# A written-out order of TensorE's jobs in place of a dispatch rule, in a fused attention and feed-forward kernel

## The chip, the cores and the metric

One core of a Trainium2 chip. The metric is the device time of one execution in microseconds (us), the median of several runs. The span in a profile is the time from the first to the last instruction of one profiled execution; the timed value is 1.7 to 2.2 us longer.

## The reference

Sigmoid attention for 8 batches of 12 heads, 448 positions, 64 wide; then a feed-forward stage on the 3584 x 768 result, with the activation h cos(h):

```python
scores = scale * np.matmul(q, k.transpose(0, 1, 3, 2)) - np.log(S)
attn = 1.0 / (1.0 + np.exp(-scores))
x = np.matmul(attn, v)              # then (batch, head, position) -> 3584 rows of 768
h = x @ w_in                        # 768 -> 2048
g = h * np.cos(h)
out = g @ w_out                     # 2048 -> 768
```

## The kernel before

The kernel is built by a small event simulation that runs when the program is made. It has a clock, assumed durations for every kind of job, pools of buffers and PSUM banks, and decides step by step what each engine is sent next. The chip then sees five fixed lists of instructions, one for each engine, with semaphores between them. Nothing is decided at run time.

The jobs, with the letters used below: **T**, a transpose of k or q of a slab (four heads of one batch; there are 24 slabs) on TensorE, only for the first slabs, the others are transposed by DMA; **S**, a score job, 64x64 matmuls on quarters of the array, evicted by ScalarE with a sigmoid; **AV**, attention times v, 28 such matmuls; first-batch products, 128x128; **group products**: the second big multiplication, and from batch 1 on the first as well, use seven products of half-size blocks in place of eight (a Strassen-like scheme), P1 to P7, whose results VectorE combines. ScalarE computes the cosine as a sine, with another activation table than the sigmoid's: the trace has 40 table loads of 1283 ns, and at 28 of them ScalarE stands no more than 0.02 us before and 0.02 after, so 1.3 us in all.

The dispatch rule for TensorE:

```python
def try_pe():
    if busy("pe"):
        return
    g = pick_group()
    n_s = S_can()
    if not visit[0]:
        left = max(0.0, free_at["act"] - now[0]) + sum(a[0] for a in act_q)
        visit[0] = (g is None or n_s >= S_VISIT or (n_s >= 1 and left < ACT_LEFT)
                    or T_pick() is not None or (AV_ok() and n_s >= 1))
    if visit[0]:
        if n_s:          start_S(); return
        if AV_ok():      start_AV(); return
        n = T_pick()
        if n is not None: start_T(n); return
        visit[0] = False
    ...                                   # (cut) else the next product of an open group
    start_group(g)
```

Copies out of PSUM go to a queue of VectorE; ScalarE takes one when the queue is long enough and VectorE is busy:

```python
elif ACT_COPIES and len(dve_q) >= DVE_LONG and busy("dve"):
    ...                                   # (cut) pick a copy that needs no second operand
    fn(1)
    run("act", dur, ACT_SEEN, fin, "copy")
```

The constants that steer it (some of them):

```python
MOST = {"raw": 4, "v": 3, "T": 6, "sig": 9, "hs": 12, "cs": 4, "st": 6}   # buffers by kind
N_PE_T = 7                # slabs transposed on TensorE
ORDER = "a1 b1 k2 v0 k1 a2 b2 v1 i0 q5 v2 k3 i2 i1 v3 q3 i3 k4 q4 o0 k5 v5 v4 o1 o2 o3"   # loads
DVE_LONG = 4
```

## Time and profile before

391.76 us (391.56 to 391.93, three runs).

| | before |
|---|---|
| span of the profiled run | 389.8 us |
| TensorE, VectorE, ScalarE busy | 367.3, 326.8, 261.1 us |
| changes between the array's forms, counted in the built list | 183 |
| activation table loads | 40 |
| first seven-product group starts | 70.5 us |

How to read it: TensorE is busy 94% of the span, so only three things can shorten it: less work in the busy time, fewer holes, or holes that move beside something that must wait anyway.

### The profile page before, as it was taken

The numbers are of one execution on the slowest core, as the hardware profiler recorded it, in microseconds if no ns is written. First come the engines' busy times: TensorE is split into PE (matmuls) and PEld (weight loads), VectorE is DVE, ScalarE is ACT, GpSimd is POOL, SyncE is SP. The second block draws the span as 40 slices with busy tenths as digits, with TensorE's granted clock in tenths as the row PEclk, the third lists the DMA queues.
The fourth block names the chain that finished last, engine by engine and source line by source line (L and its number), as shares of the span: only waits on it lengthen the run. The fifth ranks groups of instructions, "written<-read, shape, count | busy, mean of one in ns | idle before, by whom it ended". The sixth has DMA issues, their size and how long they took to land. (4 is left out here: it accounts for less than half of the span.)

```text
span 389.8 us, 9568 instructions
## 1 busy us (share of the span) xinstructions
PE 367.3 (94%) x3860; PEld 249.6 (64%) x3860; DVE 326.8 (84%) x641; ACT 261.1 (67%) x301; POOL 108.5 (28%) x132
## 2 busy tenths in 40 slices
PE   5888996899999999999999999999999999999995
PEld 3666574665567656765856765966566667967563
DVE  3346679999889897997997699999789899999962
ACT  4954899899787388788898249369988294542100
POOL 6767424264170044317044040041200000000000
PEclk9969999999999999999999999999999999999999
DMA  9999999999699399699999967483940203003333
GB/s 184 165 203 204 204 205 162 135 103 123 143 132 132 73 100 169 83 84 174 115 139 129 100 114 72 93 66 59 170 51 2 65 19 82 3 0 82 75 88 81
DMA packets 121484, 42.70 MB, mean 110 GB/s; under 512 B 96864, under 2 KB 121440, under 8 KB 121440
## 3 DMA queue, kind: packets, MB, share of 16 engines
q0 software_dynamic: 79840, 22.36, 57.6%
q1 hardware_dynamic: 41056, 19.28, 24.1%
q8 instruction: 30, 0.49, 0.5%
q10 hardware_dynamic: 544, 0.46, 0.4%
q14 instruction: 14, 0.11, 0.1%
HBM read 45.61 MB, written 11.01 MB: 145 GB/s over the span
## 5 line engine op out<-in xcount | busy, mean ns | idle before, releaser
L1118 ACT ACTIVATE u<-ps 128x896 f16<-128x896 f32 (+3 forms) x180 | 144.7, 872 | 31.8 <-PE ps L1109 28.2
L1232 DVE TENSOR_TENSOR u<-ps,u 128x448 f32<-128x448 f32 (+1 forms) x210 | 122.6, 595 | 21.5 <-PE ps L1283 14.8
L1248 DVE TENSOR_TENSOR g<-u 128x448 f16<-128x448 f32 (+6 forms) x170 | 74.2, 482 | 0.0
L1205 PEld LDWEIGHTS <-wi 128*128 128x128 f16 x672 | 62.0, 98 | 15.3 <-issue 12.4
L1235 ACT ACTIVATE u<-u 128x896 f16<-128x896 f32 x61 | 54.6, 942 | 21.3 <-issue 10.7
L1078 DVE COPY u<-ps 128x448 f32<-128x448 f32 (+6 forms) x102 | 58.7, 583 | 9.5 <-PE ps L1084 4.9
L1283 PEld LDWEIGHTS <-g 128*128 128x128 f16 x448 | 42.7, 98 | 29.7 <-issue 4.8
L1283 PE MATMUL ps<-wob,g 128*128 128x384 f16 x336 | 61.6, 326 | 0.1
L1205 PE MATMUL ps<-x,wi 128*128 128x224 f16 x504 | 59.5, 259 | 1.7 <-DVE u L1232 1.3
L1109 PE MATMUL ps<-u 64*64 64x448 f16 (+2 forms) x756 | 55.3, 354 | 2.4 <-ACT u L1118 1.7
L1016 POOL DMA_DIRECT2D u<-in_v_dram x24 | 17.7, 736 | 141.7 <-PE ps L1133 84.1
L1205 PEld LDWEIGHTS <-wis 128*128 128x128 f16 x504 | 46.8, 98 | 8.5 <-issue 6.5
L1283 PEld LDWEIGHTS <-sm 128*128 128x128 f16 x336 | 31.9, 98 | 23.5 <-issue 3.8
L1235 ACT ACT_TABLE_LOAD x20 | 25.7, 1283 | 28.4 <-DMA out_dram<-u 13.9
L1283 PE MATMUL ps<-wot,sm 128*128 128x384 f16 x224 | 41.7, 326 | 0.2 <-DVE sm L1268 0.2
L1205 PE MATMUL ps<-xs,wis 128*128 128x224 f16 x336 | 40.8, 259 | 1.0 <-DVE xs L1057 1.0
L1133 PE MATMUL ps<-u 64*64 64x448 f16 (+2 forms) x756 | 39.7, 347 | 1.6 <-ACT u L1118 1.6
L1078 DVE CAST x<-ps 128x448 f16<-128x448 f32 (+2 forms) x42 | 24.9, 617 | 16.6 <-PE ps L1133 14.7
L1109 PEld LDWEIGHTS <-u 64*64 64x64 f16 x756 | 20.4, 109 | 27.5 <-issue 24.4
L1010 POOL DMA_DIRECT2D u<-in_q_dram x34 | 33.2, 977 | 14.4 <-PE ps L1133 6.6
L1010 POOL DMA_DIRECT2D u<-in_k_dram x34 | 33.5, 986 | 4.4 <-PE ps L1084 1.4
L1133 PEld LDWEIGHTS <-u 64*64 64x64 f16 x756 | 22.7, 112 | 13.3 <-issue 4.4
(45 smaller groups left out, 277.1 us busy)
## 6 DMA issues: line engine op xcount, KB each, us to landing
out_dram<-u SPq DMA_DIRECT2D x112, 96.0 KB, 2.2
u<-in_v_dram POOLq DMA_DIRECT2D x24, 224.0 KB, 4.6
u<-in_k_dram POOLq DMA_DIRECT2D x34, 112.0 KB, 4.9
u<-in_q_dram POOLq DMA_DIRECT2D x34, 112.0 KB, 5.1
wi<-in_moe_w_in_dram POOLq DMA_DIRECT2D x16, 192.0 KB, 8.0
wob<-in_moe_w_out_dram POOLq DMA_DIRECT2D x4, 768.0 KB, 15.9
u<-in_k_dram POOLq DMA_DIRECT2D x6, 224.0 KB, 8.9
u<-in_q_dram POOLq DMA_DIRECT2D x4, 224.0 KB, 8.5
```

The source lines that it names most:

```text
L1010: self.nc.gpsimd.dma_start(out=self.u[:, buf, :].rearrange("p (j y d) -> p y j d", j=NJ, y=2)[:, y], in_=self.heads(self.src[i], s)[:, y]. ...
L1016: self.nc.gpsimd.dma_start(out=self.u[:, buf, :].rearrange("p (y n) -> p y n", y=2), in_=self.heads(self.v, s))
L1078: self.nc.vector.tensor_copy(out=out, in_=in_)
L1109: self.nc.tensor.matmul(out=self.ps[64 * x : 64 * x + 64, bks[y], w * n : w * n + w], lhsT=kT[64 * y : 64 * y + 64, j, x, :], rhs=qT[64 * ...
L1118: self.nc.scalar.activation(out=self.u[:, slot, 0 : 2 * n * w].rearrange("p (y t) -> p y t", y=2), in_=self.two(self.ps, bks, slice(0, n * ...
L1133: self.nc.tensor.matmul(out=self.ps[64 * y : 64 * y + 64, bks[x], 0:w], lhsT=self.rows(vb)[64 * x : 64 * x + 64, y, j, :], rhs=sg[64 * x : ...
L1205: self.nc.tensor.matmul(out=self.ps[:, bk, HS * e : HS * e + HS], lhsT=lhs(d)[:, f0 + 128 * e : f0 + 128 * e + 128], rhs=rhs(d), start=(na ...
L1232: self.nc.vector.tensor_tensor(out=o, in0=ps, in1=a, op=mybir.AluOpType.add)
L1235: self.nc.scalar.activation(out=self.u[:, cslot, :].rearrange("p (e t) -> p e t", e=2), in_=self.h2(hb), func=mybir.ActivationFunctionType ...
L1248: self.nc.vector.tensor_tensor(out=self.g[:, fc, t : t + w], in0=self.h1(hb)[:, a : a + w], in1=self.u[:, cslot, S * e + a : S * e + a + w ...
L1283: self.nc.tensor.matmul(out=self.ps[:, bk, 0:HD], lhsT=lhs[:, i, :], rhs=self.wo[w][:, i, :], start=(name in OPENS and i == 0), stop=(i == 7),
```

## The change

Its intent: TensorE's order is no longer found by the rule but written down as a string of 650 letters (S, A for AV, T, W for a warm-up matmul, a to d for groups into the hidden layer, x to z for output groups). The builder takes the next letter, waits on its own clock until that job may start, and starts it. Nobody reads the result of the warm-up matmuls. Many constants change with it, and the last pair's second stores go to ScalarE's queue.

```diff
-MOST = {"raw": 4, "v": 3, "T": 6, "sig": 9, "hs": 12, "cs": 4, "st": 6}
-N_PE_T = 7
+MOST = {"raw": 8, "v": 2, "T": 8, "sig": 15, "hs": 14, "cs": 5, "st": 10}
+N_PE_T = 6
-ORDER = "a1 b1 k2 v0 k1 a2 b2 v1 i0 q5 v2 k3 i2 i1 v3 q3 i3 k4 q4 o0 k5 v5 v4 o1 o2 o3"
+ORDER = "v2 k2 k1 v0 b2 a1 b1 q4 k3 a2 q5 o0 k4 v1 q3 i0 k5 i1 i2 v3 i3 o1 o3 o2 v4 v5"
-DVE_LONG = 4
+DVE_LONG = 1
+PLAN = (
+    "TTSTTSSSSSWWSASSTTSSTSASTTSSTSSSTTSSSSATSSTSSASSSTSASSSaSTSSAbSSabcSSdSSdabcSSSaAcSSSdSWScdSaSabSSbb"
+    "cdcaadbcddAcAbabScacbSbaSccSSaccSSbacbaabxbASSxxxxSSxxxSSxxSSSxxxSSASxdSSddSSASddadbdabaSSabababSScb"
+    ...                                   (cut: five more lines)
+)
+    def follow():
+        c = PLAN[step[0]]
+        if c == "S":
+            if S_pick() is None or not bank_pairs() or not can("sig", 1):
+                return
+            start_S()
+        ...                                   (cut: A, T, W and the group letters)
+        step[0] += 1
     def try_pe():
         if busy("pe"):
             return
+        if PLAN:
+            follow()
+            return
-                            outq.append(
+                            on_act = hh == 1 and p == NPAIR - 1
+                            (outa if on_act else outq).append(
```

Cut as well: a model of TensorE's clock in the builder (its author's estimate), changed assumed durations and safety margins, other priorities in VectorE's queue, and an identity matrix cleared by VectorE in place of GpSimd.

More of the change, by code (lines that the diff above doesn't have):

```diff
@@ L28 @@
 LEAST = {"raw": 2, "v": 1, "T": 2, "sig": 7, "hs": 4, "cs": 1, "st": 4}
-MOST = {"raw": 4, "v": 3, "T": 6, "sig": 9, "hs": 12, "cs": 4, "st": 6}
-N_PE_T = 7
+MOST = {"raw": 8, "v": 2, "T": 8, "sig": 15, "hs": 14, "cs": 5, "st": 10}
+N_PE_T = 6
 SIN_BURST = 6
-LEAD = 700
+LEAD = 800
 MAX_GROUPS = 3
-S_VISIT = 3
-ISSUE_IL, COST_IL = 1.5, 1.0
+S_VISIT = 2
+ISSUE_IL, COST_IL = 0.98, 0.8
 HOLD = 0
 ACT_COPIES = True
-ORDER = "a1 b1 k2 v0 k1 a2 b2 v1 i0 q5 v2 k3 i2 i1 v3 q3 i3 k4 q4 o0 k5 v5 v4 o1 o2 o3"
-SAFE_RAW, SAFE_IL, SAFE_T = 3.0, 3.5, 1.0
-FIRST_AT = (3.3, 3.8, 4.6, 5.4)
-PR = {"AV": 2, "T": 1, "xsum": 2, "sum": 1, "sum_later": 2, "g": 2}
-ACT_LEFT = 0.7
-DVE_LONG = 4
+ORDER = "v2 k2 k1 v0 b2 a1 b1 q4 k3 a2 q5 o0 k4 v1 q3 i0 k5 i1 i2 v3 i3 o1 o3 o2 v4 v5"
+SAFE_RAW = 1
+SAFE_IL = 2.5
+SAFE_T = 1.5
+SAFE_L = 0.7
+H0 = 0.45
+H1 = 0.48
+FIRST_AT = (3.55, 4.15, 5.15, 5.85)
+PR = {"AV": 0, "T": 0, "xsum": 1, "sum": 2, "sum_later": 3, "g": 1}
+ACT_LEFT = 0.2
+IDENT_AT = 1.6
+WARM_N = 1
+WARM_SPAN = 1.7
+WARM_SHARE = 0.6
+PHASE = 1.47
+PLAN = (
+    "TTSTTSSSSSWWSASSTTSSTSASTTSSTSSSTTSSSSATSSTSSASSSTSASSSaSTSSAbSSabcSSdSSdabcSSSaAcSSSdSWScdSaSabSSbb"
+    "cdcaadbcddAcAbabScacbSbaSccSSaccSSbacbaabxbASSxxxxSSxxxSSxxSSSxxxSSASxdSSddSSASddadbdabaSSabababSScb"
+    "SASbcSScyySScyySSyyySSyyySASyySSyyzcazczzzSAczzSSSdzzzSSddzSSzdSSSzdaddaSAaazbbSSaabaSSASxSSbxbSSbcx"
+    "xcxxcxSScxxxccxxcxSSASbxSSSdySSydySSddyddyyydySSASaSbybSayayyybaySASabcbaSczzbcaScczdcSbzzzcdzdzSASS"
+    "dzdzSSddzzSSSzzxxSSASaxaaxxaSxxaaSSaxSSSxxSASSxxxSSASxbSSSbbcbyybyccbdccyybddyadycdyycyadadaySSyyaya"
+    "SSASabSSSzzzbSSzzzbzSASSzzxSSzxzcdczzzbccbAxxxbdcxxbxcddxxcaaxdadbxdccaabxccbabxcyybayccyyyydbzdydyy"
+    "byydzzzzdzzddzyzzyzzzxxxxxxxzxxxxyyxyyyyyxyyxyyyyy"
+)
+DVE_LONG = 1
 TRACE = None
@@ L49, in n_buf @@
     return int(kb / 1.75)
-PRODUCTS = ("P1", "P6", "P2", "P7", "P5", "P4", "P3")
+PRODUCTS = {"m1s": ("P1", "P6", "P2", "P7", "P5", "P4", "P3"), "m2": ("P1", "P6", "P2", "P7", "P5", "P4", "P3")}
 BANK_OF = {"P1": "a", "P2": "a", "P6": "b", "P7": "b", "P4": "b", "P5": "c", "P3": "c"}
@@ L171, in schedule @@
     mode = ["full"]
+    active = []
     m1_next = [0, 0, 0]
+    m1_seq = [0]
+    step = [0]
     m1_left = [NFC] * B
@@ L189, in schedule @@
     groups = []
-    outq = []
+    outq, outa = [], []
     def pieces(s, i):
@@ L252, in schedule @@
     l_i = [0]
-    dma_at = [4.85]
+    dma_at = [3.85]
+    slow = [True]
     flying = [0]
@@ L284, in try_load @@
         dma_at[0] = max(dma_at[0], now[0] + (4.4 if kind == "wo" else 1.1)) + dur
+        if slow[0] and dma_at[0] > 12.5:
+            slow[0] = False
+            dma_at[0] += 1.7
         def done():
@@ L298, in done @@
                 wo_got[a] = 1
-        at(dma_at[0] + 1.65, done)
+        at(dma_at[0] + 1.65 + SAFE_L, done)
     def try_sp():
@@ L326, in try_sp, with pe_run, activity, try_warm @@
                 at(dma_at[0] + 2.4, fin)
+    WINDOW = 3.413
+    clock = {"end": PHASE, "sum": 0.0, "next": 0.0, "full": False}
+    def pe_run(dur, sw, done, tag):
+        while clock["end"] <= now[0]:
+            clock["full"] = clock["sum"] >= WINDOW * (H0 if clock["full"] else H1)
+            clock["end"] += WINDOW
+            clock["sum"], clock["next"] = clock["next"], 0.0
+        real = dur if clock["full"] else 2 * dur
+        room = max(0.0, clock["end"] - now[0] - sw)
+        part = min(1.0, room / real)
+        clock["sum"] += dur * part
+        clock["next"] += dur * (1 - part)
+        active.append((now[0] + sw, now[0] + sw + real))
+        run("pe", real + sw, PE_SEEN, done, tag)
+    def activity():
+        lo = now[0] - WARM_SPAN
+        while active and active[0][1] < lo:
+            active.pop(0)
+        return sum(b - max(a, lo) for a, b in active) / WARM_SPAN
+    def try_warm():
+        if now[0] < IDENT_AT or not banks or m2_next[0] >= NPAIR or activity() >= WARM_SHARE:
+            return
+        start_warm()
+    def start_warm():
+        log.append((now[0], "W"))
+        bk = bank()
+        ops.pe_warm(bk, WARM_N)
+        pe_run(WARM_N * 0.0555, switch("full"), lambda: None, "warm")
+        unbank(bk)
     def switch(m):
@@ L409, in done @@
             act_q.append((t_act(2 * w * len(js)), lambda: ops.act_sig(bks, w, len(js), slot), fin))
-        run("pe", TILE * len(js) * w / S + switch("tile"), PE_SEEN, done, f"S{s}.{js[0]}")
+        pe_run(TILE * len(js) * w / S, switch("tile"), done, f"S{s}.{js[0]}")
     def start_AV():
@@ L448, in done @@
                 )
-        run("pe", NJ * TILE * w / S + switch("tile"), PE_SEEN, done, f"AV{s}")
+        pe_run(NJ * TILE * w / S, switch("tile"), done, f"AV{s}")
     def start_T(n):
@@ L471, in done @@
             dve_q.append((PR["T"], t_dve16(w), lambda e: ops.cp_T(e, bk, buf, js), fin, t_act(w)))
-        run("pe", 0.113 * (js[1] - js[0]) + switch("T"), PE_SEEN, done, f"T{s}.{i}")
+        pe_run(0.113 * (js[1] - js[0]), switch("T"), done, f"T{s}.{i}")
     def m1_open():
@@ L514, in open_m1 @@
             m1_next[:] = [b, 0, i + 1] if i < 3 else [b + 1, 0, 0]
+        g["id"] = "abcd"[m1_seq[0] % 4]
+        m1_seq[0] += 1
         groups.append(g)
@@ L520, in open_m2 @@
         m2_next[0] += 1
-        g = {"kind": "m2", "p": p, "k": 0, "half": 0, "bk": {}, "got": set(), "st": take("st", 4)}
+        g = {"kind": "m2", "id": "xyz"[p % 3], "p": p, "k": 0, "half": 0, "bk": {}, "got": set(), "st": take("st", 4)}
         groups.append(g)
@@ L547, in ready @@
             return True
-        name = PRODUCTS[g["k"]]
-        if name in OPENS and len(banks) <= (0 if g["k"] else HOLD):
+        name = PRODUCTS[g["kind"]][g["k"]]
+        if name in OPENS and len(banks) <= (0 if g["k"] or PLAN else HOLD):
             return False
@@ L568, in start_group @@
     def start_group(g):
+        log.append((now[0], "G", g["id"]))
         if g["kind"] == "m1c":
@@ L612, in done @@
                     )
-            run("pe", NDC * MM448 * w / S + switch("full"), PE_SEEN, done, f"m1c{b}.{i}")
+            pe_run(NDC * MM448 * w / S, switch("full"), done, f"m1c{b}.{i}")
             return
         k = g["k"]
-        name = PRODUCTS[k]
+        name = PRODUCTS[g["kind"]][k]
         if name in OPENS and not g["half"]:
@@ L639, in start_group, with queue, fin @@
         what = GIVES[name]
+        def queue(job):
+            if what == "c22" and "u3" not in g["got"]:
+                g["later"] = job
+            else:
+                dve_q.append(job)
+                if what == "u3":
+                    fin3 = job[3]
+                    def fin():
+                        fin3()
+                        if "later" in g:
+                            dve_q.append(g.pop("later"))
+                    dve_q[-1] = job[:3] + (fin, job[4])
         def done():
@@ L658, in done @@
                 alone = what in ("s1", "c11")
-                dve_q.append(
+                queue(
                     (
@@ L684, in fin @@
                         for hh in range(2):
-                            outq.append(
+                            on_act = hh == 1 and p == NPAIR - 1
+                            (outa if on_act else outq).append(
                                 (
-                                    lambda hh=hh: ops.sp_out(p, r, h, hh, buf),
+                                    lambda hh=hh, a=on_act: ops.store(p, r, h, hh, buf, a),
                                     (lambda: give("st", [buf])) if hh else None,
@@ L692, in done @@
                 alone = what in ("s1", "c11")
-                dve_q.append(
+                queue(
                     (
@@ L701, in done @@
                 )
-        run("pe", dur + switch("full"), PE_SEEN, done, f"{g['kind']}.{name}")
+        pe_run(dur, switch("full"), done, f"{g['kind']}.{name}")
     def lead():
@@ L724, in why @@
         for g in groups:
-            n = PRODUCTS[g["k"]] if "got" in g else "c"
+            n = PRODUCTS[g["kind"]][g["k"]] if "got" in g else "c"
             if "got" in g and n in NEEDS and NEEDS[n] not in g["got"]:
@@ L747, in schedule @@
     visit = [False]
+    def follow():
+        if step[0] >= len(PLAN):
+            return
+        c = PLAN[step[0]]
+        if c == "S":
+            if S_pick() is None or not bank_pairs() or not can("sig", 1):
+                return
+            start_S()
+        elif c == "A":
+            if not AV_ok():
+                return
+            start_AV()
+        elif c == "T":
+            n = T_pick()
+            if n is None:
+                return
+            start_T(n)
+        elif c == "W":
+            if now[0] < IDENT_AT or not banks:
+                return
+            start_warm()
+        else:
+            g = [g for g in groups if g["id"] == c]
+            if g and not ready(g[0]):
+                return
+            if not g:
+                if not banks:
+                    return
+                if c in "abcd":
+                    k1 = m1_open()
+                    assert c == "abcd"[m1_seq[0] % 4]
+                    if k1 is None:
+                        return
+                    g = [open_m1(k1)]
+                else:
+                    assert c == "xyz"[m2_next[0] % 3]
+                    if not m2_open():
+                        return
+                    g = [open_m2()]
+            start_group(g[0])
+        step[0] += 1
     def try_pe():
         if busy("pe"):
+            return
+        if PLAN:
+            follow()
             return
@@ L777, in try_pe @@
                 why()
+            try_warm()
             return
@@ L801, in try_act @@
             run("act", dur + t, ACT_SEEN, fin, "sig")
+        elif outa:
+            fn, fin = outa.pop(0)
+            fn()
+            dma_at[0] = max(dma_at[0], now[0] + 0.3) + 0.28
+            run("act", 0.1, ACT_SEEN, lambda: None, "out")
+            at(dma_at[0] + 2.4, fin)
         elif ACT_COPIES and len(dve_q) >= DVE_LONG and busy("dve"):
@@ L910, in schedule @@
         at(FIRST_AT[n], got)
+    at(IDENT_AT, lambda: None)
     while True:
@@ L924, in schedule @@
             heapq.heappop(events)[2]()
-    assert pair_done[0] == NPAIR and not outq, (
+    assert pair_done[0] == NPAIR and not outq and not outa, (
         now[0], pair_done, len(outq), m1_next, m2_next, len(S_JOBS), len(AV_JOBS), banks, held, len(bufs), groups, len(hs_ready), wisum, wosum, T_JOBS
@@ L1091, in pe_T, with pe_warm @@
                 )
+    def pe_warm(self, bk, n):
+        self.nc.tensor.matmul(
+            out=self.ps[:, bk, 0 : 128 * n],
+            lhsT=self.ident,
+            rhs=self.ident.unsqueeze(1).to_broadcast([128, n, 128]),
+            start=True,
+            stop=True,
+            skip_group_check=True,
+        )
     def cp_T(self, eng, bk, buf, js):
@@ L1294, in ev_m2, with store @@
         self.combine(eng, what, self.ps[:, bk, 0:HD], c11, c12, c21, c22)
-    def sp_out(self, p, r, h, hh, buf):
+    def store(self, p, r, h, hh, buf, on_act):
         t = 256 * p + 128 * r + 64 * hh
         b, j = divmod(t // 64, NJ)
-        self.nc.sync.dma_start(
+        eng = self.nc.scalar if on_act else self.nc.sync
+        eng.dma_start(
             out=self.out_rows[b, j, :, HD * h : HD * h + HD], in_=self.uf[64 * hh : 64 * hh + 64, buf, 0:HD]
@@ L1319 @@
     ctx.enter_context(tc.manual_schedule())
-    make_identity(nc, ops.ident)
+    nc.vector.memset(ops.ident, 0.0)
     nc.vector.memset(ops.warm, 0.0)
+    make_identity(nc, ops.ident, nomemset=True)
     nc.scalar.activation(
```

## The prediction

> **What bounds the kernel now.** I read the page first, for the busiest engine and for where its row has holes.
>
> ```profile
> PE 367.3 (94%) x3860; PEld 249.6 (64%) x3860; DVE 326.8 (84%) x641; ACT 261.1 (67%) x301; POOL 108.5 (28%) x132
> PE   5888996899999999999999999999999999999995
> PEclk9969999999999999999999999999999999999999
> DMA  9999999999699399699999967483940203003333
> ```
>
> TensorE is the bound, but not evenly: nearly all holes lie in the first eight slices (78 us), where the DMA row is also at 9. So I took the busy time in stretches of 10 us.
>
> ```profile
> 0.00:10.00 10.00, 5.28 (x81) 3.38 (x83) 3.83 (x11) 4.33 (x7) 6.96 (x15) 1.00 0.93 183
> 10.00:20.00 10.00, 8.29 (x206) 5.89 (x206) 3.45 (x7) 9.05 (x16) 6.77 (x12) 0.93 1.18 166
> 20.00:30.00 10.00, 9.00 (x160) 6.59 (x160) 5.22 (x9) 5.54 (x11) 6.18 (x10) 0.73 1.25 204
> ...
> 60.00:70.00 10.00, 6.36 (x89) 3.94 (x91) 9.23 (x16) 8.71 (x11) 5.02 (x6) 0.83 1.86 151
> ```
>
> The columns are the stretch, its length, busy time of PE, PEld, DVE, ACT and POOL, granted clock, DMA share, GB/s. From 60 to 70 us TensorE works 6.4 us of 10, partly at half clock, and VectorE is full. A busy TensorE is not always a productive one, so the third view is its timeline.
>
> ```profile
> 74.06 0.74 PE L1205 MATMUL ps<-x,wi 128*128 128x224 f16 x6
> 74.64 0.74 PE L1205 MATMUL ps<-xs,wis 128*128 128x224 f16 x6
> ...
> 79.83 0.74 PE L1205 MATMUL ps<-x,wis 128*128 128x224 f16 x6
> 80.50 0.38 PE L1109 MATMUL ps<-u 64*64 64x448 f16 x4
> 80.81 0.75 PE L1205 MATMUL ps<-xs,wis 128*128 128x224 f16 x6
> ```
>
> Starts tell more than durations, since neighbours overlap. Six products followed by their like take 0.58 us (74.06 to 74.64); followed by a score job (four 64x64 matmuls) 0.67. The score job, 0.19 when another one of its kind follows, takes 0.31 when a full-array product follows. So each change between the 128x128 and the 64-row form of the array costs about 0.093 us, both ways.
>
> With start-to-start times of all matmuls (96 ns for 128x224, 162.5 for 128x384, 82.5 and 109 for 192 and 256 columns, 190 for four 64x448) I split the 389.8 us span: 3.9 before the first matmul; 327.8 of matmuls at full clock (112.9 group products into the hidden layer, 127.2 output products, 18.4 first-batch products, 32.0 scores, 32.0 attention times V (AV), 5.3 transposes); 183 changes of form x 0.093 = 17.0; 36.4 of waits and half clock; 4.7 after the start of the last matmul. Of the 36.4, 23.4 lie before 70.5 us and 13.0 after it. At 70.5 us the first seven-product group starts; from there TensorE has 287.2 us of matmuls and 158 changes left. Check: 70.5 + 287.2 + 14.7 + 13.0 + 4.7 = 390.1.
>
> [...] 14 transposes take 0.96 us before 11 us and 0.58 after, and the records have half clock for 6.8 us from 17.9 and for 3.4 us from 65.7. [...] (a load at 56.80 ends at 58.08, the next activation starts at 58.10).
>
> **The change part by part.** Both kernels are lists fixed when they are built; the old one came from a greedy rule, the new one is written out. So I compared the built instructions, not the rules.
>
> Work: the group, score and AV matmuls are the same. Slab 6 is now transposed by DMA: 28 transposes fewer, 14 pairs x 54 ns = -0.75 us. Three warm-up matmuls come in (+0.16 us), for the clock.
>
> Changes of form: 183 become 151, so -32 x 0.093 = -3.0 us. Scores now mostly come in twos and threes: single-score visits fall from 25 to 13.
>
> Opening: this is the largest part and partly chosen. By the first group the new list has 39.2 us of matmuls and 31 changes (2.9 us) behind it, the old 40.8 us and 25. The old one had its last first-batch product at 60.7 us, then fell into transposes that waited for VectorE, and needed ten more us for 3.5 us of work; that stretch went cold. The new list spreads transposes and AVs between the first-batch products and has only one AV and twelve such products between the last-but-one AV and the first group. Its limit is then the load stream: same bytes (w_in, w_out, 18 slabs), with v of slabs 4 and 5 now last. In the trace the load just behind these same bytes lands at 60.2 us; one load at 1.1 us less gives 59.1. The old stream paused 2.3 us around 5 us, because only four raw buffers were allowed (now eight). I take one to two us of that back: v5 at 57.5 to 58. Then an AV (1.33 us) and its copies (0.6) and latencies: first group at about 61 us. TensorE's own minimum does not bind: 3.9 + 39.2 + 2.9 + about 3.5 for half clock = 49.5.
>
> After the first group: 288.2 us of matmuls (1.0 more than the old), 120 changes = 11.2 (3.5 less). Waits: of the old 13.0 us some 8.7 are gaps over 150 ns, most of them on VectorE; 4.3 are small steps that any order has. VectorE is relieved: 37 group/x copies of 448 columns (0.616 each), 7 of 384 (0.55), 8 of the first batch (5 x 0.69, 3 x 0.555) and 2 transpose copies (0.62) leave it, 33 us; it falls to about 294. ScalarE takes the copies (about 28 us at its 0.49 to 0.61 each) but loads 26 tables in place of 40: -14 x 1.283 = -18.0. It stands near 271. I choose 7 us for the new waits: the 4.3 plus about 2.7.
>
> End: in the trace the last two stores are issued at 386.06 and 386.58 on one queue; on two they go together: -0.5, so 4.2 for 4.7.
>
> Sum of the span: 61 + 288.2 + 11.2 + 7 + 4.2 = 371.6. The timed median lies 1.95 above the span (391.76 against 389.8), so 373.5 us. As differences: opening -9.5, work +1.0, changes -3.5, waits -6, stores -0.5: -18.5, rounded from 391.8.
>
> **Rivals.** *The loads hold the opening.* v is now held to two buffers, so v4 and v5 can be issued only when earlier AVs are done, and ScalarE feeds those. For it: the DMA row is at 9 through 60 us. Against: eight loads may fly ahead, a lead of 8 us. If it holds, the group starts at 66 to 68: 379 to 381 us. *A fixed order blocks at its head.* The list was made with assumed durations; where a load or a copy comes late, TensorE waits although other work is ready. Against: the old list is just as fixed. It would add 3 to 6 us: 377 to 380. *ScalarE becomes the bound.* It takes copies that TensorE's banks wait for, behind sigmoids of 0.92 us and table loads. Against: 271 of 372 us busy. Local waits of perhaps 3 us. *The gaps were the only gain*: the opening stays, only form changes and stores count: 391.8 - 3.0 - 0.75 - 0.5 = 387.5, "same".
>
> **Range and chances.** Each of the first three rivals adds 3 to 7 us and two may come together: up to 382. If the waits fall to the bare 4.3 and the group starts at 58, 368; so 367 to 382. The bound for "faster by over 2%" is 384, ten us from the point; only a failed opening together with new waits crosses it: 0.88 faster, 0.10 same, 0.02 slower.
>
> **What would show it.** Right: the first seven-product group at 59 to 63 us; no slice of TensorE below 8 after the second; VectorE near 294, ScalarE near 271 us busy; 151 changes; the two last stores issued at the same moment. Wrong: the group after 66 us; a half-clock stretch between 25 and 70 us; gaps of TensorE over 0.15 us after the opening adding to more than 5 us; ScalarE named as releaser of most of them.

## More of the kernel before

Runs that are quoted were fast unless the text says otherwise.

The page's chain of waits, followed back from the last instruction, says who held the end:

```profile
PE 19%; DVE 9%; issue 1%; ACT 0%; DVEq 0%
```

These are shares of the span by engine. They add to 29% because the chain goes back only to 274 us; in that last part TensorE and VectorE take turns.

## The result, and the profile after

375.72 us (374.85 to 376.63, four runs) against 391.66 (390.91 to 391.93, four runs beside it): 15.9 us less. The ratio is 0.9596, 95% interval 0.9568 to 0.9624: faster. Ratios here are the mean time of one kernel's fast runs over that of the other's in the same rounds, so not quite the ratio of the medians quoted.

The page of the changed kernel, same rows as the prediction showed of before:

```profile
PE 356.6 (95%) x3835; PEld 249.4 (67%) x3835; DVE 299.4 (80%) x588; ACT 268.4 (72%) x339; POOL 110.7 (30%) x133
PE   4989899899999999999999999999999999999995
PEclk9999999999999999999999999999999999999999
DMA  9999999989999799699959929979922111011333
```

The hole at slices 7 and 8 is gone, and no slice between the first and the last is below 8. The share of TensorE hardly rose (94 to 95%): a span gets shorter with its busy time when both go. The chain of waits:

```profile
PE 76%; DMA 12%; DVE 7%; POOL 2%; issue 1%; ACT 1%; DVEq 0%; POOLq 0%; ACTq 0%
```

It now goes back to the start and lies on TensorE for three quarters of the span; VectorE, a third of the part traced before, is down to 7%. Of the 12% on DMA, 36.5 us lie in the first 50.1: the chain goes there through loads of v, of w_in (twice) and of w_out, which lands at 50.1. The stretches of 10 us (columns as in the prediction):

```profile
0.00:10.00 10.00, 4.55 (x67) 3.04 (x68) 3.00 (x9) 4.66 (x8) 8.05 (x16) 1.00 0.93 190
10.00:20.00 10.00, 9.10 (x213) 6.91 (x213) 4.40 (x10) 7.85 (x15) 5.55 (x9) 1.00 1.34 201
20.00:30.00 10.00, 8.48 (x214) 5.92 (x214) 4.28 (x8) 8.91 (x18) 5.82 (x10) 1.00 1.25 204
...
60.00:70.00 10.00, 8.07 (x101) 5.51 (x90) 9.48 (x18) 8.31 (x13) 8.47 (x10) 1.00 1.27 125
```

From 60 to 70 us TensorE now works 8.1 us of 10, before 6.4. What happened there is plainest in the two timelines (start, length, engine, line, operation, count, and in brackets the idle time before and who ended it). Before, where L1161 is a first-batch product, L1084 a transpose, L1109 a score job, L1133 an AV:

```profile
57.50 3.45 PE L1161 MATMUL ps<-x,wi 128*128 128x256 f16 x30
60.88 0.58 PE L1084 MATMUL ps<-ident,u 128*64 128x128 f16 x14
63.08 0.58 PE L1084 MATMUL ps<-ident,u 128*64 128x128 f16 x14 [1.62 <-DVE u L1078]
63.85 0.38 PE L1109 MATMUL ps<-u 64*64 64x448 f16 x4 [0.19 <-ACT u L1118]
...
67.09 2.80 PE L1133 MATMUL ps<-u 64*64 64x448 f16 x28 [1.24 <-ACT u L1118]
69.65 0.80 PE L1109 MATMUL ps<-u 64*64 64x448 f16 x12
70.52 1.31 PE L1205 MATMUL ps<-x,wi 128*128 128x224 f16 x12
```

After (L1308 first-batch product, L1280 AV, L1256 score job, L1352 group product):

```profile
50.84 8.33 PE L1308 MATMUL ps<-x,wi 128*128 128x256 f16 x72
59.10 1.52 PE L1280 MATMUL ps<-u 64*64 64x448 f16 x28
60.55 0.83 PE L1308 MATMUL ps<-x,wi 128*128 128x256 f16 x6
61.31 1.52 PE L1280 MATMUL ps<-u 64*64 64x448 f16 x28
62.76 0.83 PE L1308 MATMUL ps<-x,wi 128*128 128x256 f16 x6
63.42 0.74 PE L1352 MATMUL ps<-x,wi 128*128 128x224 f16 x6
...
67.82 1.89 PE L1352 MATMUL ps<-xs,wis 128*128 128x224 f16 x18 [1.69 <-DVE xs L1194]
```

Before, all first-batch products were done at 61 us, and what was left until the first group was a chain transpose, copy, scores, sigmoid, AV, each waiting for another engine; the AV ran at half clock (2.80 us for what takes 1.52; the granted clock was 0.50 from 66.3 to 69.7 us). After, the transposes and scores of batch 1 are done earlier, and the last two AVs lie between first-batch products, so from 46.6 us to the first group TensorE has no gap over 0.15 us. That group starts at 63.4 us, 7.1 earlier; a new wait of 1.7 us follows at 66.1.

The whole difference of the spans, counted from the starts of all matmuls as in the prediction (matmuls at full clock; changes of form x 0.093 us; what is left over are waits and half clock):

| us | before | after | difference |
|---|---|---|---|
| up to the first group: matmuls | 40.75 | 39.21 | -1.54 |
| changes of form | 2.3 (25) | 2.9 (31) | +0.56 |
| waits and half clock | 23.5 | 17.5 | -6.05 |
| from there on: matmuls | 287.05 | 288.01 | +0.96 |
| changes of form | 14.7 (158) | 11.2 (120) | -3.53 |
| waits | 12.84 | 7.95 | -4.89 |
| before the first matmul, and after the start of the last | 8.6 | 8.2 | -0.44 |
| sum, the span | 389.8 | 374.9 | -14.9 |

The changes counted are those between 128x128 and 64x64; 22 and 21 more, to and from transposes, stand in the waits before the first group. The profiled run of the changed kernel was the slowest of its four, so the difference of the medians is 1 us larger than that of the spans.

### The profile page after: what moved, and what is told of

Its sections match the earlier page's. It is cut to its first block, busy times and chain, and to the rows that moved or that the text cites. A ratio compares the mean times of both kernels' runs of the same rounds, so it can differ in the third digit from the quotient of the medians.

```text
span 374.9 us, 9531 instructions
## 1 busy us (share of the span) xinstructions
PE 356.6 (95%) x3835; PEld 249.4 (67%) x3835; DVE 299.4 (80%) x588; ACT 268.4 (72%) x339; POOL 110.7 (30%) x133
## 4 chain that ended last, share of the span: by engine, by line
PE 76%; DMA 12%; DVE 7%; POOL 2%; issue 1%; ACT 1%; DVEq 0%; POOLq 0%; ACTq 0%
PE ps L1430 32%; PE ps L1352 26%; PE ps L1256 8%; PE ps L1280 7%; DMA wi<-in_moe_w_in_dram 4%; DMA wob<-in_moe_w_out_dram 4%; DMA u<-u 2%; DVE g L1395 2%; DVE u L1379 2%; DMA u<-in_v_dram 2%; PE ps L1308 1%; DVE xs L1194 1%; POOL u L1144 1%; PE ps L1221 1%; DVE wot L1205 1%
## 5 line engine op out<-in xcount | busy, mean ns | idle before, releaser
L1379 DVE TENSOR_TENSOR u<-ps,u 128x448 f32<-128x448 f32 (+1 forms) x210 | 120.5, 598 | 25.0 <-PE ps L1430 15.8
L1352 PEld LDWEIGHTS <-wi 128*128 128x128 f16 x672 | 62.8, 98 | 10.9 <-issue 7.6
L1153 POOL DMA_DIRECT2D u<-in_v_dram x24 | 17.7, 739 | 161.7 <-PE ps L1256 109.1
L1430 PE MATMUL ps<-wob,g 128*128 128x384 f16 x336 | 64.0, 326 | 0.0
L1352 PE MATMUL ps<-x,wi 128*128 128x224 f16 x504 | 59.5, 259 | 0.2 <-ACT u L1211 0.2
L1256 PE MATMUL ps<-u 64*64 64x448 f16 (+2 forms) x756 | 54.9, 349 | 4.9 <-DMA u<-u 1.7
L1352 PEld LDWEIGHTS <-wis 128*128 128x128 f16 x504 | 47.5, 98 | 10.1 <-issue 6.1
L1215 DVE COPY u<-ps 128x448 f32<-128x448 f32 (+7 forms) x62 | 35.3, 574 | 17.0 <-PE ps L1430 7.5
L1211 ACT ACTIVATE u<-ps 128x448 f32<-128x448 f32 (+3 forms) x48 | 25.2, 532 | 30.2 <-PE ps L1352 11.6
L1430 PE MATMUL ps<-wot,sm 128*128 128x384 f16 x224 | 42.8, 326 | 0.0
L1352 PE MATMUL ps<-xs,wis 128*128 128x224 f16 x336 | 40.6, 259 | 1.8 <-DVE xs L1194 1.7
L1256 PEld LDWEIGHTS <-u 64*64 64x64 f16 x756 | 20.2, 108 | 27.9 <-issue 24.1
L1280 PE MATMUL ps<-u 64*64 64x448 f16 (+2 forms) x756 | 37.3, 334 | 0.2 <-DMA u<-in_v_dram 0.2
L1147 POOL DMA_DIRECT2D u<-in_k_dram x36 | 35.4, 986 | 1.2 <-ACT u L1211 0.7
L1147 POOL DMA_DIRECT2D u<-in_q_dram x36 | 35.1, 977 | 0.2 <-issue 0.2
L1215 DVE CAST x<-ps 128x448 f16<-128x448 f32 (+2 forms) x30 | 18.3, 622 | 17.9 <-PE ps L1280 16.3
L1280 PEld LDWEIGHTS <-u 64*64 64x64 f16 x756 | 22.3, 109 | 10.2 <-issue 1.3
```

The source lines that it names most:

```text
L1147: self.nc.gpsimd.dma_start(out=self.u[:, buf, :].rearrange("p (j y d) -> p y j d", j=NJ, y=2)[:, y], in_=self.heads(self.src[i], s)[:, y]. ...
L1153: self.nc.gpsimd.dma_start(out=self.u[:, buf, :].rearrange("p (y n) -> p y n", y=2), in_=self.heads(self.v, s))
L1211: self.nc.scalar.activation(out=out, in_=in_, func=mybir.ActivationFunctionType.Copy, bias=0.0, scale=1.0)
L1215: self.nc.vector.tensor_copy(out=out, in_=in_)
L1256: self.nc.tensor.matmul(out=self.ps[64 * x : 64 * x + 64, bks[y], w * n : w * n + w], lhsT=kT[64 * y : 64 * y + 64, j, x, :], rhs=qT[64 * ...
L1280: self.nc.tensor.matmul(out=self.ps[64 * y : 64 * y + 64, bks[x], 0:w], lhsT=self.rows(vb)[64 * x : 64 * x + 64, y, j, :], rhs=sg[64 * x : ...
```

## The experiments

Twelve kernels ran. The experiments fall into two kinds, and the difference turned out to matter more than anything else. In the first kind the source is changed and the builder runs anew, so every list may change. In the second the builder believes that nothing was changed, and only what it sends to one engine differs; the other lists stay as they are, which was checked on the built lists; the order of the instructions in the traces agrees.

My theory before them: the gain is in the order, which takes holes out of the opening and lifts copies off VectorE, and in fewer changes of form; the clock and the stores are small. Rivals: the new constants alone do it; the warm-up matmuls (the clock) do it; the stores.

### Kind one: the builder runs anew

**The rule with the new constants.**

```diff
-PLAN = ( ... )
+PLAN = ""
-            try_warm()
```

> The changed kernel with its written-out list taken away: the old dispatch rule orders TensorE again, with all the new constants (load order, buffers, copies to ScalarE, last stores on two queues), no warm-up matmuls. Built, it has 167 changes of form (before 183, changed kernel 151), 34 table loads (40, 26), 618 VectorE instructions (640, 586). Theory 1 (the written order carries the gain): opening and waits stay as before, only changes of form (-1.5), the transposes (-0.75) and the stores (-0.5) count: 386 to 390 us. Theory 2 (the constants carry it, any order would do): 375 to 379 us. Between, 380 to 385, both do.

Measured: 419.8 and 424.8 us in its two fast runs, ratio 1.0785 (the median with two slow runs is 426.3). Its profiled run was slow, so its trace is not used. Neither theory's number holds. The rule with these constants makes the kernel 31 us slower than it was before, so the constants are not a gain that the list merely rides on. In the built lists the rule puts 50.8 us of matmuls ahead of the first group, where the list puts 39.2.

**The list for the opening only.**

```diff
-        if PLAN:
+        if step[0] < len(PLAN):        # PLAN cut after its 114th letter
             follow()
             return
...                                    (cut)
-            try_warm()
```

> The written-out list up to the first seven-product group (its first 114 entries, the same 39.2 us of matmuls and 31 changes), from there the dispatch rule with the new constants. 157 changes, 30 table loads, 602 VectorE instructions. If the opening alone carries what the list gains, the time is within 1 us of the changed kernel (375 to 377) and the first group starts at 63.4. If the later part of the list also counts (waits 7.9 to about 13, six changes more, 0.6), it is 380 to 382 us with the first group at the same 63.4.

Measured: 426.6 us (425.1 to 428.1), ratio 1.0894. The first group starts at 63.0 us, as expected, so the opening is carried by the first 114 letters with these constants. After it the waits are 56.3 us in place of 8.0, with 157 changes of form in place of 151. I had expected 5 more. With these constants the later part of the list is worth some 50 us over the rule, with the other lists made anew to fit.

**No warm-up matmuls.**

```diff
-    "TTSTTSSSSSWWSASSTTSSTSAS..."
+    "TTSTTSSSSSSASSTTSSTSAS..."      (all three W taken out)
```

> The changed kernel without its three warm-up matmuls; the list is otherwise the same. If they keep or bring the full clock, a half-clock stretch of 3.4 us or more appears before 50 us and the time rises by 1 to 2 us. If the work around them does it alone, nothing changes: within 0.5 us of 375.7.

Measured: 393.4 us (392.7 to 395.0), ratio 1.0052: all of the gain gone, by taking out three matmuls that nobody reads. The trace has half clock from 22.2 to 29.0 and from 39.2 to 46.1 us, and once more for 3.4 us from 261.1 (mean granted clock of the run 0.976). The first group starts at 73.8 us, 10.4 later than with the warm-ups, and 15.3 us of waits follow it in place of 8.0. The waits of TensorE that stand out:

```profile
25.02 0.96 PE L1221 MATMUL ps<-ident,u 128*64 128x128 f16 x14 [3.82 <-DMA u<-in_q_dram]
...
41.66 1.12 PE L1308 MATMUL ps<-x,wi 128*128 128x192 f16 x6 [3.98 <-DVE u L1215]
```

A transpose waits for a load and a first-batch product for VectorE, 4 us each; the half clock begins after each of the first two waits set in. TensorE's list differs only by the three matmuls, as far as line and shape go; but VectorE's list differs over a stretch of some 320 rows and ScalarE's in 49 lines. In the trace GpSimd's order is the same, and those of VectorE, ScalarE and SyncE's DMA queue are not. So this run can't say what the warm-ups do: it changed several lists at once. That is what the second kind is for.

**No copies on ScalarE.**

```diff
-ACT_COPIES = True
+ACT_COPIES = False
```

> The changed kernel with every copy left on VectorE, none on ScalarE; the list is the same, 151 changes. VectorE gets 68 instructions more (654 against 586), some 37 us, and would be busy about 337 us. If the relief of VectorE is what took the waits after the opening from 13.0 to 7.9 us, the time is 381 us or more, with waits of TensorE on VectorE after 70 us; if the order alone did, it stays within 2 us of 375.7.

Measured: 413.4 us (412.3 to 414.1), ratio 1.0555. In the direction expected, and far more; but again lists were made anew: in the trace TensorE's and GpSimd's orders are the same, but more than the copies moved in VectorE's, and SyncE's DMA queue differs too.

What the four share: they all lose, by 17 to 51 us. The builder's own clock, the sum of what it assumes, ends at 382.8 for the kernel before, 374.3 for the changed one, and 416, 416, 393 and 418 for these four (its return value, run without a chip); the spans measured were 389.8 and 374.9, and 423.4, 392.5 and 412.1 for the last three. So the loss is no accident of the chip: the builder saw it too. The kernel before and the changed one look like points where list and constants fit each other. The same figures show one thing more. By its own clock, whose assumptions changed too, the builder gained 8.5 us with the change (382.8 to 374.3), and the chip 14.9: it ran 7.0 us behind the builder before, and 0.6 after. So some 6 us of the gain are a plan that the chip keeps better, and not a shorter plan; what in the new assumptions does it was not tested.

### Kind two: the lists are kept

**The warm-ups not sent.**

```diff
         bk = bank()
-        ops.pe_warm(bk, WARM_N)
         pe_run(WARM_N * 0.0555, switch("full"), lambda: None, "warm")
```

> The builder keeps its whole plan as in the changed kernel, so the lists of all engines are the same instruction by instruction; only the three warm-up matmuls are not sent to TensorE. Theory 1 (the 17.7 us of the run without warm-ups came from the lists being made anew on other assumed times, a half-clock stretch included in them): 375 to 377 us, at most one half-clock stretch. Theory 2 (the warm-ups themselves keep the clock, and the clock costs 17 us): 385 us or more.

Measured: 376.7 us (376.1 to 377.3), ratio 0.9601. The lists of the other four engines are the same row by row. Theory 1 holds: against 375.7 us and 0.9596 with overlapping intervals, the three matmuls are worth about a microsecond or nothing. The profiled run has half clock from 31.0 to 34.4 us (mean granted clock of the run 0.995) and its first group at 64.0. That stretch can't be put down to the missing warm-ups: the profile of the control below, which has them, shows half clock from 30.4 to 33.8 us (granted clock 0.50), has its first group at 63.3, and is no slower (375.3).

**54 changes of form more, and its control.** 27 times after the opening, a single small matmul is sent between two full-array products, into a free bank. Once it uses a quarter of the array, once the whole.

```diff
+        if g["kind"] != "m1c" and mode[0] == "full":
+            extra[0] += 1
+            if extra[0] % 8 == 0 and bank_pairs():
+                ops.pe_extra(bank_pairs()[0])
+    def pe_extra(self, bk):
+        self.nc.tensor.matmul(out=self.ps[0:64, bk, 0:64],
+            lhsT=self.ident[0:64, 0:64], rhs=self.ident[0:64, 0:64], ...)
+    # the control: [0:128, bk, 0:64], ident[0:128, 0:128], ident[0:128, 0:64]
```

> Lists of all engines as in the changed kernel; after the opening 27 single 64x64 matmuls of 64 columns are sent between two full-array products, into a free bank, so 54 changes of form more. If a change costs 0.093 us and TensorE is the bound there, 27 x (0.186 + 0.03 to 0.1) = 5.8 to 7.7 us more than the changed kernel: 381.5 to 383.5. If it hides beside waits, less than 3 us more.

> The control of the run with 54 changes of form more: the same 27 places and banks, but a 128x128 matmul of 64 columns, which keeps the form. If it is the form that costs, 27 x about 0.03 = 0.8 us over the changed kernel; if it is the extra instruction or the wait for its bank, as much as the other (6 us or more).

Measured: 381.5 us (380.4 to 382.4) with the quarter, 375.6 (375.3 to 378.1) with the whole array; the changed kernel itself had 375.7. The timeline of the first (L1236 is the extra matmul):

```profile
79.00 0.74 PE L1367 MATMUL ps<-xs,wi 128*128 128x224 f16 x6
79.67 0.21 PE L1236 MATMUL ps<-ident 64*64 64x64 f16 x1
79.82 0.82 PE L1445 MATMUL ps<-wob,g 128*128 128x384 f16 x4
```

and of the control:

```profile
78.92 0.74 PE L1367 MATMUL ps<-xs,wi 128*128 128x224 f16 x6
79.50 0.19 PE L1236 MATMUL ps<-ident 128*128 128x64 f16 x1
79.53 0.81 PE L1445 MATMUL ps<-wob,g 128*128 128x384 f16 x4
```

From the six products' start to the output product's it takes 0.82 us with the quarter and 0.61 with the whole array: 0.21 for two changes. Over the runs (381.46 - 375.63) / 54 = 0.108 us for each by the medians, 0.098 by the means, and by the spans (378.9 - 373.5) / 54 = 0.100. That a change of form costs about 0.1 us, fully on the path, is shown, and the extra instruction by itself costs nothing that can be seen.

**Copies sent to VectorE.**

```diff
-                fn(1)
+                fn(1 if now[0] < 63 else 0)
                 run("act", dur, ACT_SEEN, fin, "copy")
```

> The builder keeps its plan and the order of TensorE; after the opening the copies that it gives to ScalarE are sent to VectorE instead, at the same place in time (58 instructions more there, about 33 us, 330 us busy in all). If taking them off VectorE is what cut the waits after the opening from 12.8 to 8.0 us, the time is 380 us or more and the new waits name VectorE; if the order of TensorE alone did, it stays within 2 us of 375.7.

Measured: 396.4 us (395.3 to 397.4), ratio 1.0107 (1.0071 to 1.0143): 20.7 us more than the changed kernel, and 1% more than the kernel before. TensorE's order is the same. Its waits after the first group grow from 8.0 to 26.5 us (by the starts). The view of who waited for whom, for TensorE (waited for: us in total, times, longest):

```profile
PE ps L1352 <- DVE u L1379: 4.4, 9, 1.9
...
PE ps L1352 <- DVE u L1215: 3.1, 2, 2.7
PE ps L1430 <- DVE u L1379: 3.0, 6, 1.1
```

The changed kernel has none of these three after 70 us; its only entry there is one transfer of 1.7 us. VectorE is busy 327.0 us in this run, as in the kernel before (326.8). So this order of TensorE's jobs gives its gain with VectorE at 299 us, and not with the 58 copies put back. How much of the 20.7 us is the load and how much the place is not shown: nobody chose where the copies stand in VectorE's list.

**The last stores on one queue.**

```diff
-                            on_act = hh == 1 and p == NPAIR - 1
+                            on_act = False
```

> The changed kernel with the last pair's stores all on the one queue again. If the second queue saves the issue time of the last store (0.52 us in the trace of the kernel before), the tail after the last matmul's start is 4.7 in place of 4.3 us and the time 0.3 to 0.6 us longer: 376.0 to 376.3. If the landing hides it, no difference.

Measured: 377.2 us (375.9 to 377.8, five runs), ratio 0.9615 against 0.9596; the intervals overlap (0.9593 to 0.9637 and 0.9568 to 0.9624). The tail after the start of the last matmul is clearer: 5.19 against 4.31 us. One queue:

```profile
367.01 4.97 SPq L1447 DMA_DIRECT2D out_dram<-u  x8
...
369.68 0.56 DVE L1379 TENSOR_TENSOR u<-ps,u 128x384 f32<-128x384 f32 x1 [0.74 <-PE ps L1430]
```

The changed kernel, two queues:

```profile
368.24 3.72 SPq L1447 DMA_DIRECT2D out_dram<-u  x5
368.90 3.10 ACTq L1447 DMA_DIRECT2D out_dram<-u  x3
...
370.91 0.56 DVE L1379 TENSOR_TENSOR u<-ps,u 128x384 f32<-128x384 f32 x1 [0.74 <-PE ps L1430]
```

The last issue ends 371.98 - 370.24 = 1.74 us after the last combination on one queue, 372.00 - 371.47 = 0.53 on two. Of those 1.2 us, 0.9 show in the tail.

**Warm-ups that fill the opening.** 20 before the first transpose, ten more in the gaps of the first 10 us.

```diff
+    def fill():
+        n = {0: 20, 1: 3, 2: 5, 8: 2}.get(step[0], 0)
+        for _ in range(n):
+            ops.pe_warm(banks[-1], 1)
...                                    (cut: called before each S and each T)
```

> Lists as in the changed kernel, but 20 more warm-up matmuls before the first transpose and 10 more in the gaps of the first 10 us. If the half clock up to 14.8 us holds the opening, the full clock comes at 5 to 8 us, the first group 1 to 3 us earlier and the time falls by as much. If loads and ScalarE pace the opening, the clock comes earlier and the first group stays at 63 to 64 us, the time within 0.7 us.

Measured: 377.5 us (376.8 to 379.1), ratio 0.9632. The full clock came at 5.6 us, was lost again from 9.0 to 15.8 (mean granted clock of the run 0.991), and the first group came at 65.3, later and not earlier. Not a gain; the loss of 1.7 us is at the edge of what the intervals separate (0.9608 to 0.9655).

**The kernel before with its gaps filled.** Its own lists, and 52 warm-ups where its builder has TensorE idle.

```diff
         if g is None:
+            if 1.6 < now[0] < 75 and banks and now[0] > filled[0] + 0.15:
+                filled[0] = now[0]
+                ops.pe_warm(banks[-1], NW)        # NW = 3: 384 columns
             return
```

(and two more places between 13.5 and 24 us.)

> The kernel before with its own lists, and 52 warm-up matmuls sent where the builder has TensorE idle before 75 us. If the half-clock stretches (18.5 to 25.4 and 66.3 to 69.7 us) are what makes its opening long, they shrink and the time falls by 3 to 5 us: 387 to 389. If the waits for loads and copies pace it, 391 to 392 with or without them.

Measured: 392.0 us (391.0 to 393.0, twelve runs) beside 391.8 of the kernel before (nineteen runs), ratio 1.0004, interval 0.9989 to 1.0019. The former half-clock stretches (columns as above, the clock is the third from the right):

```profile
18.50:25.40 6.90, 5.69 (x112) 3.22 (x112) 1.27 (x3) 5.81 (x11) 3.50 (x6) 1.00 1.25 204
66.30:69.70 3.40, 3.27 (x50) 1.65 (x46) 3.40 (x7) 3.29 (x6) 0.74 (x1) 1.00 2.08 128
```

The clock is full from 7.9 us to the last matmuls, and the time doesn't move by more than 0.2%. So half clock is not what made the time of the kernel before. In this profile the first group starts 0.8 us earlier (69.7 against 70.5), but the twelve runs together show nothing of it. The fill takes 7.9 us of TensorE's time itself, at full clock, so a small cost of the half clock may hide behind it.

**Two sums before two differences.** The new wait at 66.1 us is for sums of x on VectorE. VectorE's timeline in the changed kernel (L1185 two late differences of weights, L1194 the sums):

```profile
63.30 1.83 DVE L1185 TENSOR_TENSOR wi<-wi,wi 128x1536 f16<-128x1536 f16 x2 [0.42 <-PE ps L1308]
65.04 1.69 DVE L1395 TENSOR_TENSOR g<-u 128x448 f16<-128x448 f32 x3
66.65 0.50 DVE L1194 TENSOR_TENSOR xs<-x 128x672 f16<-128x672 f16 x1
```

The edit holds the two differences back until two sums were sent:

```diff
-                        lambda k=k: ops.dve_xsum(b % N_X, b % N_XS, k),
+                        lambda k=k: send_xsum(b, k),      # after k == 1: send what was put off
-                    (0 if k == 2 else 4, t_dve16(1536), lambda k=k, c=c: ops.dve_wisum(k, c), fin, None)
+                        lambda k=k, c=c: put_off.append((k, c)) if k == 2 else ops.dve_wisum(k, c),
```

> The builder's plan unchanged; only on VectorE the two late weight differences (1.83 us together, sent at 63.3 us in the changed kernel) are sent after the first two sums of x of batch 1 and not before them. In the changed kernel TensorE waits 1.69 us at 66.1 us for these sums. If VectorE's order makes that wait, P6 of the first groups starts 1.5 to 1.9 us earlier and the time falls by 0.8 to 1.8 us, to 374 to 375 (some may come back at P7, which needs the late differences). If it is paced by something else (ScalarE's copies of x), the wait stays and so does the time.

Measured: 374.9 us (373.5 to 375.3, six runs), ratio 0.9560 (0.9530 to 0.9590) against 0.9596: best of all kernels, though the intervals overlap. Group product P6 starts 65.66 - 63.12 = 2.5 us after the first group, before 67.82 - 63.42 = 4.4. The wait before it is gone; 0.6 us of it come back before a score job that waits for ScalarE. The step is shown by the trace, its 0.9 us only made likely by the times.

## Why the prediction was right or wrong, point by point

The time was predicted as 373.5 us (367 to 382) and came as 375.7; the gain as 18.3 us and came as 15.9. By the spans, whose terms were predicted, the miss is 3.3 us (371.6 and 374.9), nearly all of it in the first two terms that went wrong, the opening (2.4) and the waits after it (1.0). The 1.95 us put on top of the span compared the median with another run's span; that run itself, at 391.61 us, lies 1.8 above it. Term by term:

- **Work and changes of form.** As counted: +1.0 and -3.5 us after the first group, 151 changes in the trace. The price of a change was read as 0.093 us "both ways"; the lines shown with it give 0.67 - 0.58 = 0.09 into the 64-row form and 0.31 - 0.19 = 0.12 out of it, 0.105 on average. Adding 54 measured 0.098 to 0.108 and showed that it lies wholly on the path. At 0.105 some 0.5 us of the 4.9 that the table gives to waits belong to changes of form.
- **Opening, -9.5 predicted, -7.1 measured.** The mechanism was right: transposes and AVs between first-batch products close the hole from 61 to 70 us. The step that was mis-sized is "Its limit is then the load stream", with the first group at about 61 us. In the trace v of slab 5 landed at 56.3 us, earlier than the 57.5 to 58 assumed, and the group came 7.1 us later, where 3 to 3.5 had been allowed: from 46.6 us on TensorE was full with first-batch products, scores and the two AVs. My "TensorE's own minimum does not bind" (49.5 us) left out the waits: 17.5 us of waits and half clock lie before the first group. So TensorE did not stand waiting for the end of the load stream.
- **What paces the opening stays open.** Loads earlier in the stream still may: the chain of waits lies on them for 36.5 of the first 50.1 us, TensorE itself waits 1.0 us for w_in before 37.8, and in ten of the eleven profiles with this order of TensorE's jobs in the opening the first group starts 7.2 to 7.6 us after v of slab 5, whether that lands at 55.8 us or at 58.0 (in the run without warm-ups it is 15.1). No run moved the loads alone.
- **Half clock as part of the story.** I put the hole of the kernel before partly on a "stretch that went cold". Cold it was, but filling it with dummy matmuls kept the clock up and did not change the time (391.99 against 391.82 us). The times I gave for the two half-clock stretches, 17.9 and 65.7 us, were 0.6 too early; they are 18.5 and 66.3. The granted clock in them was 0.50. In the opening the first record of full clock is at 11.7 us (14.8 in the changed kernel); 14 transposes take 0.96 us at 9.9 us and 0.58 at 12.3. What takes the full clock away was not shown: from 15.1 to 18.5 us TensorE works 2.28 us and its longest wait is 0.43, from 62.9 to 66.3 it works 1.99.
- **Waits after the opening, 13 to 7 us predicted, 12.8 to 8.0 measured.** That the copies on ScalarE are needed for it is shown by sending 58 back (+20.7 us, with waits that name VectorE). One wait among the 8.0 us, 1.8 at 111 us for a DMA transpose, is absent from the runs with the warm-ups not sent and with the control matmuls, so it varies from run to run.
- **VectorE and ScalarE.** 294 and 271 us predicted, 299.4 and 268.4 measured. I subtracted 33 us of durations, but instructions that follow each other closely overlap (two of 0.62 us take 1.15), so busy time fell by 27.4; the 58 copies sent back added 27.6.
- **Stores.** 0.5 us predicted from one issue of 0.52. The tail came as 4.3 us for 4.7; in the changed kernel the undone step cost more, 0.9, as its last issue then ends 1.74 us after the last combination, where two queues leave 0.53.
- **Rivals.** The first group did not come at 66 to 68 us, as it should have if v of slabs 4 and 5 came late; that loads hold the opening in another place is not excluded (above). A new local wait did appear (1.7 us for the sums of x), on VectorE and not on ScalarE. "A fixed order blocks at its head" did not come true for this list on this chip, but the four rebuilt kernels show how close it lies: three matmuls out of the list, and the builder made lists that lose 17.7 us.
- **Signs.** No slice of TensorE but the first and the last is below 8, the changes are 151, and the last issues of the two queues end within 0.04 us, as said for "right". The first group, at 63.4 us, lies just outside 59 to 63. One sign of "wrong" came true: gaps over 0.15 us after the opening, counted by starts, add to 5.4 us (8.8 before), 1.8 of them the wait that varies. A half-clock stretch between 25 and 70 us is not in this profile; the run with the warm-ups not sent and the control have one, at no cost that can be seen.

What stays open: how the 6 us of waits won in the opening divide among the order of loads, the buffers and the order of jobs. Changing one of these alone lets the builder change every list, so the gain can be placed in time and on engines, but not shared out over the lines of the diff.

## What to carry to other kernels

When a program is built by a scheduler, changing one input remakes every list; to learn what one part is worth, keep the lists and change only what is sent. Count changes of array form in the built list and price them from start-to-start times (about 0.1 us each here): fewer changes, above all by score jobs in twos and threes, saved some 3.5 to 4 us here. A low clock is not yet a cost: filling the half-clock stretches of the kernel before bought nothing (391.99 us against 391.82), while with 27 us of copies put back on VectorE the tight order lost all of its gain. And a plan is worth what the chip keeps of it: compare the builder's end time with the measured span.
